# Value sums taken from the attention's own value tiles, in a kernel whose order of work is one written line

## The chip, the cores and the metric

One Trainium2 chip, one core. The metric is device microseconds of one execution. Six things run beside each other on the core: TensorE (PE in the tables, with PEld for its weight loads), VectorE (DVE), ScalarE (ACT), GpSimd (POOL), SyncE (SP, which here only issues DMAs), and the DMA engines themselves. Each of the five engines works through its own instructions strictly in the order in which they were written.

## The reference

Local attention with a coarse summary of the whole sequence, then two dense blocks. Batch 2, 8 heads, 768 positions, head width 64. Each query sees the positions less than 16 away and, besides, 24 summaries of 32 positions each: the maximum of the keys and the mean of the values.

```python
k_sum = k.reshape(B, H, nb, block, D).max(axis=3)      # nb 24, block 32
v_sum = v.reshape(B, H, nb, block, D).mean(axis=3)
scores_l = where(|i - j| < 16, scale * q @ k.T, -1e9)
scores_s = scale * q @ k_sum.T + log(block)
a = softmax(concat([scores_l, scores_s]))
x = a @ concat([v, v_sum])                             # 1536 tokens x 512
h = x @ w_in;  g = max(h, 0) + log1p(exp(-|h|))        # 512 -> 2048
x2 = g @ w_out                                         # 2048 -> 512
out = (((x2 @ w1) * (x2 @ w2)) @ w3) @ w_out2          # 512 -> 1024 -> 512
```

## The kernel before

**Steps and the line.** The work is cut into 2,060 named steps. Every step has an engine, a function that issues its instructions, the steps it needs, and the buffers that it takes and gives back. `LINE` (from line 59) names all steps once, in one order; the last lines of the kernel walk through it and call each function. So the line fixes the order on every engine, SP's queue of DMA issues included. `Order.order` (line 38) only asserts, while the program is built, that needs come first and that no pool of buffers is overdrawn; it issues nothing. The numbers handed to `add` and `padd` (costs, due times, `lead`) were for the search that wrote the line and issue nothing either. The waits on the chip come from the data and the buffers: an instruction waits for what it reads, and the first write to a buffer waits for the last use of the tile that had it.

**Attention.** Twelve tiles of 128 queries, u = 0 to 11, six for each batch element. For tile u: `kw{u}` copies two windows of 96 keys out of the loaded keys `kl`, `ks{u}` adds the 24 block maxima (`km`), `A{u}` makes the scores on TensorE, `max{u}e` (DVE) and `exp{u}e` (ACT) do the softmax in 8 pieces, `inv{u}` (DVE) and `norm{u}h` (POOL) divide, `T{u}h` transposes on TensorE into one of two "a" banks, `at{u}h` copies that out (h = 0 on DVE, h = 1 on ACT), `AV{u}` multiplies with the values, and `xh{u}`, `xl{u}` split the result into two parts for the dense blocks.

**Values.** `vw{u}` loads the two windows of 96 value rows of tile u into rows 0 to 95 of a tile with 120 rows; there are four such tiles. Rows 96 to 119 are the 24 block means. These come from a second load of all the values: `vl{b}{i}`, four transfers of 384 rows each, into a buffer of the "xt" pool (3 buffers). `vs{b}s{i}` multiplies them with a selection matrix (1/32 where a row belongs to a block) on TensorE, 12 products for each half batch. `vsT{b}` copies the sums out on ACT. For batch element 0, `vsu0` turns them back into rows on TensorE and `vs0_h`, `vs1_h` copy them into the tiles of u = 0 and 1; all others go through DRAM (`vss{b}` stores, `vs{u}` loads).

**Dense blocks.** `H` (x @ w_in), `sa` to `lo` (softplus and split), `X` (g @ w_out), products for a Strassen-like scheme (`Ph`, `Pp`), `wm` (w3 @ w_out2), `AB` and `O` (the last product, 24 steps for each column m of four). Every weight passes through a load `l…`, four conversions `ca` to `cd` on ACT and DVE, and `ce`, `c…` on ACT and POOL. At the end `Oo{c}{m}` copies the bank of rows c, m out (odd m on DVE, even m on ACT, into one of 6 "tmp" buffers) and `Os{c}{m}` stores it from SP.

**Order around the change, before.** SP: kl0 ml il q0 kl1 vl00 q1 vw3 sell q2 vw2 kl2 vw0 vl10 vw1 kl3 lw_in0 lw_in2 lw_in1 vl01 q5 q4 q3 vl11. TensorE: A1 A0 vs0s0 A2 T01 T00 T10 T11 T20 T21 vs0s1 vsu0 A3 AV1 AV0 A4 A5 T30. The end of the line: O22_3 Oo10 O23_3 Os10 Oo23 Os23.

Of the kernel before, what the change touches and what calls it, by code (L numbers as in the profile page):

```python
# [59 lines left out]
kl0 sz ml z il busy q0 kl1 vl00 q1 vw3 sell q2 vw2 kl2 vw0 vl10 km0 kw1 vw1 kl3 kw0 lw_in0 lw_in2 lw_in1 km1 kw5 ks0 ks1 ks5 vl01 A1 A0 kw2 max10 q5  # L60
max11 exp10 max12 exp11 vs0s0 max13 kw4 q4 ks2 exp13 max00 exp12 max01 exp00 max02 exp01 max03 max04 exp02 A2 max05 exp03 ks4 max14 exp05 max15 max16
exp15 kw3 q3 max20 exp16 max21 max22 exp14 max23 exp04 max24 max25 exp24 max26 exp25 max27 ks3 exp27 km2 exp23 exp26 exp22 exp20 max17 exp21 max06
max07 exp06 inv2 exp07 norm20 exp17 inv0 vl11 inv1 norm01 norm11 T01 at01 norm21 norm10 km3 norm00 T00 caw_in0 T10 cbw_in0 at10 at00 T11 ccw_in0 T20
cdw_in0 at11 at20 lw_in3 ccw_in1 T21 caw_in1 cbw_in1 at21 caw_in2 cdw_in1 vs0s1 cbw_in2 cew_in1 lw_out0 ccw_in2 vsT0 cw_in1 vss0 vsu0 cdw_in2 vs0_1
vs0_0 lw_out1 A3 vs1_1 vs1_0 cew_in2 AV1 cew_in0 max30 kw6 q6 max31 exp30 max32 max33 exp32 cw_in2 AV0 max34 vw5 exp33 max35 max36 exp34 ks6 exp31 A4
max37 cw_in0 vw4 xh0 exp37 xl0 A5 exp35 q7 kw8 max40 exp36 max41 exp40 vs2 max42 inv3 kw7 q9 exp42 max43 vs3 exp41 max44 max45 exp44 norm31 max46
exp43 max47 max50 exp47 max51 norm30 exp46 max52 max53 exp45 max54 exp53 inv4 T30 exp50 max55 T31 ks8 norm40 exp52 at30 xh1 A6 ks7 at31 vs5 norm41 xl1
# [1127 lines left out]
```

## Time and profile before

| | us |
|---|---|
| median of 3 runs | 576.73 (576.16 to 577.13) |
| the profiled execution's own time | 579.54 |
| its span, first to last instruction | 577.8 |
| TensorE busy in the span | 542.0 (94%) |
| VectorE, ScalarE, GpSimd busy | 440.1, 325.6, 183.1 |

The rows are of that one profiled execution, and their times count from the start of its span. "[8.0 <-POOL s L373]" behind a row says how long the engine had idled before it and what ended the wait. PEclk is the TensorE clock that was granted: 1.00 is 2.4 GHz, 0.50 is 1.2 GHz, and a value between is a mean over a stretch that had both.

### The profile page before, as it was taken

To read this page: it belongs to the slowest core of one execution; us is meant where nothing else is said; L and a number is where in the kernel's file an instruction comes from. 1 tells how busy PE (TensorE), PEld (TensorE's weight loads), DVE (VectorE), ACT (ScalarE), POOL (GpSimd) and SP (SyncE) were. 2 spreads that over 40 slices of the span, in tenths; PEclk is the share of its full clock that TensorE was granted. 3 is DMA by queue.
4 is the path that set the end of the run, shared out by engine and by line. 5 is a ranking of instruction groups with operands and counts; after the bars stand their busy time and mean duration, and the time that the engine had idled before them with its cause. 6 is when DMAs were issued, how large, how long until landed. Compare 5 with 4: busy or idle time off the path is not lost.

```text
span 577.8 us, 8732 instructions
## 1 busy us (share of the span) xinstructions
PE 542.0 (94%) x3118; PEld 441.3 (76%) x3118; DVE 440.1 (76%) x812; ACT 325.6 (56%) x695; POOL 183.1 (32%) x162
## 2 busy tenths in 40 slices
...
GB/s 287 334 272 168 172 111 73 180 169 196 39 145 97 233 163 130 213 243 54 238 223 108 218 250 312 307 206 174 152 127 1 19 73 0 1 1 1 1 1 145
DMA packets 35476, 84.29 MB, mean 146 GB/s; under 512 B 4552, under 2 KB 5000, under 8 KB 35432
## 3 DMA queue, kind: packets, MB, share of 16 engines
...
q8 instruction: 24, 0.39, 0.3%
q14 instruction: 20, 0.16, 0.1%
...
## 4 chain that ended last, share of the span: by engine, by line
PE 45%; DVE 19%; issue 11%; DMA 10%; ACT 9%; POOL 5%; SPq 1%; DVEq 0%; POOLq 0%; ACTq 0%
PE abps L663 19%; PE ops L183 9%; PE xps L183 9%; DVE raw L204 3%; ACT s L361 3%; DVE cv L216 3%; PE hps L183 3%; DMA raw<-in_w_dram 3%; PE wps L183 2%; DMA raw<-in_w_out_dram 2%; POOL w L231 2%; DVE gt L462 2%; DVE tm L449 2%; DMA qt<-in_q_dram 2%; POOL w L534 2%
## 5 line engine op out<-in xcount | busy, mean ns | idle before, releaser
L183 PE MATMUL xps<-gt,w 128*128 128x512 f32 x576 | 137.4, 390 | 1.1 <-DVE gt L462 1.0
L231 POOL TENSOR_TENSOR w<-cv,w 128x512 fp32r<-128x512 f32 x60 | 92.8, 1559 | 139.2 <-ACT w L227 123.9
L183 PEld LDWEIGHTS xps<-gt,w 128*128 128x128 f32 x576 | 107.8, 188 | 24.8 <-DVE gt L462 1.9
L204 DVE SCALAR_TENSOR_TENSOR raw<-raw 128x512 int32<-128x512 int32 x72 | 63.0, 880 | 12.9 <-ACT raw L200 12.6
L183 PE MATMUL hps<-xt,w 128*128 128x512 f32 x288 | 70.2, 394 | 2.0 <-DVE u L675 1.4
L183 PE MATMUL ops<-w,pt 128*128 128x512 f32 x288 | 70.0, 390 | 0.1
L216 DVE SCALAR_TENSOR_TENSOR cv<-cv,raw 128x512 int32<-128x512 int32 x72 | 64.2, 900 | 3.5 <-ACT cv L210 2.0
L183 PEld LDWEIGHTS hps<-xt,w 128*128 128x128 f32 x288 | 53.1, 188 | 14.2 <-DVE u L675 1.8
L183 PEld LDWEIGHTS ops<-w,pt 128*128 128x128 f32 x288 | 54.0, 188 | 12.1 <-DVE pt L561 0.9
L200 ACT ACTIVATE raw<-raw 128x512 int32<-128x512 uint16 x69 | 46.2, 674 | 25.7 <-DMA raw<-in_w_dram 14.7
L484 POOL DMA_DIRECT2D x_d<-xo x36 | 32.9, 1096 | 67.8 <-ACT xo L476 55.4
L675 DVE TENSOR_TENSOR u<-u,abps 128x512 f32<-128x512 f32 x42 | 28.8, 686 | 33.1 <-PE abps L663 19.2
L227 ACT CAST w<-cv 128x512 fp32r<-128x512 f32 x72 | 42.9, 619 | 18.7 <-DVE cv L216 14.8
L669 ACT COPY u<-abps 128x512 f32<-128x512 f32 x42 | 24.6, 587 | 44.7 <-PE abps L663 36.3
L183 PE MATMUL abps<-x2t,w 128*128 128x512 f32 x192 | 44.4, 389 | 0.0
L183 PE MATMUL wps<-w 128*128 128x512 f32 x192 | 44.2, 389 | 0.0
L663 PE MATMUL abps<-t,s 128*128 128x512 f32 x168 | 42.6, 392 | 0.6 <-DVE gt L462 0.6
L361 ACT ACTIVATE s<-s,sm 128x120 f32<-128x120 f32 x96 | 36.8, 386 | 8.9 <-DVE sm L355 8.7
L183 PEld LDWEIGHTS wps<-w 128*128 128x128 f32 x192 | 36.0, 188 | 7.5
L183 PEld LDWEIGHTS abps<-x2t,w 128*128 128x128 f32 x192 | 36.0, 188 | 7.5
L452 ACT ACTIVATE tm<-tm 128x512 f32<-128x512 f32 x48 | 29.4, 628 | 20.3 <-DVE tm L449 20.2
L210 ACT ACTIVATE cv<-raw 128x512 f32<-128x512 f32 x52 | 33.8, 668 | 10.3 <-DMA pk_wo<-cv 3.1
...
## 6 DMA issues: line engine op xcount, KB each, us to landing
raw<-in_w_dram SPq DMA_DIRECT2D x32, 512.0 KB
x_d<-xo POOLq DMA_DIRECT2D x36, 256.0 KB, 5.8
raw<-in_w_in_dram SPq DMA_DIRECT2D x16, 512.0 KB
raw<-in_w_out_dram SPq DMA_DIRECT2D x16, 512.0 KB
vw<-in_v_dram SPq DMA_DIRECT2D x12, 384.0 KB
raw<-in_wo_dram SPq DMA_DIRECT2D x8, 512.0 KB
kt<-in_k_dram SPq DMA_DIRECT2D x4, 768.0 KB
qt<-in_q_dram SPq DMA_DIRECT2D x12, 256.0 KB
```

The lines of the kernel that those rows point to most:

```text
L183: nc.tensor.matmul(ps, lhs(a), rhs(b), start=first and i == 0, stop=last and i == 2)
L200: nc.scalar.activation(r[:, :, 0], r.bitcast(U16)[:, :, 1], AF.Copy, bias=-(0.5 - 2.0 ** -14), scale=2.0 ** -13)
L204: nc.vector.scalar_tensor_tensor(r[:, :, 0], r[:, :, 1], -0x80000000, r[:, :, 0], ALU.bitwise_and, ALU.bitwise_or)
L210: nc.scalar.activation(f(c), h, AF.Copy, scale=2.0 ** -112)
L216: nc.vector.scalar_tensor_tensor(c, c, 3, r[:, :, 0], ALU.logical_shift_left, ALU.bitwise_or)
L227: nc.scalar.copy(w[:, 0], f(cvs[kind, i]))
L231: eng.tensor_tensor(w[:, 1], f(cvs[kind, i]), f(w[:, 0]), ALU.subtract)
L361: nc.scalar.activation(s[:, e], s[:, e], AF.Exp, bias=sm[:, 0, e:e + 1], scale=-1.0, accum_out=sm[:, 1, e:e + 1])
L452: nc.scalar.activation(tm[c, i], tm[c, i], AF.Softplus)
L484: nc.gpsimd.dma_start(x2_d[4 * c + o], xo[c, g, o], accum_op=ALU.add)
L663: nc.tensor.matmul(ps, w[:, a, (o + kk) * P:(o + kk + 1) * P], rhs(b), start=k in (1, 5, 2) and kk == 0 and n == 0, stop=kk == 1 and n == ...
L675: nc.vector.tensor_tensor(tu[z, j, d], tu[z, j, d], bank[z, j, k], ALU.add)
```

## The change

The loads `vl` and their buffers go. The block sums are now made from the window tiles `vw{u}`, which hold the same rows: of each of the two windows of a tile, one selection picks the 64 rows of its own two blocks. `vs{b}s{i}` (4 steps of 12 products) become `vss{u}` (12 steps of 8 products), each needing its `vw{u}`. The selection matrix becomes three small ones, filled by three DMAs of two numbers for each of 64 rows. The tiles of u = 4 to 7 now lie together in one "xt" buffer, held until AV7. The store that was called `vss{b}` is now `vsd{b}`. Users of buffers are told to `Order` more fully, and the whole line is another one.

```diff
-    sel_t = ap_.tile([P, 6, 32], F32, name="sel_t")
+    sel_t = ap_.tile([W, 3, 80], F32, name="sel_t")
...
-        nc.sync.dma_start(vt[b][:, 3 * i:3 * i + 3], v[b, 384 * i:384 * i + 384].rearrange("(a p) c -> p a c", p=P))
...
-                nc.tensor.matmul(vs_t[b][32 * c:32 * c + 32], sel_t[:, a], vt[b][:, a, c * P:(c + 1) * P],
-                                 start=a == 0, stop=a == 5)
+    OFFS = (0, 16, 32)
+    def sel_load(v_):
+        nc.sync.dma_start(sel_t[OFFS[v_]:OFFS[v_] + 64, v_, 46:48], sel[0:64, 0, 0:2])
+    def v_sum(t):
+        b, j = divmod(t, NT)
+        if j == 0:
             vs_t[b] = ph.tile([P, P], F32, tag="h", name="vs_t")
+        for blk, w in enumerate(wins(t)):
+            i = 2 * j + blk
+            s_ = sel_t[:, OFFS.index(64 * i - w), 46 - 2 * i:78 - 2 * i]
             for c in range(4):
+                nc.tensor.matmul(vs_t[b][32 * c:32 * c + 32], s_, vw[t][0:W, blk, c * P:(c + 1) * P],
+                                 start=i == 0, stop=i == 2 * NT - 1)
...
+        if t in (4, 5, 6, 7):
+            if t == 4:
+                four[0] = xt_p.tile([NK, 4, 2, D], F32, tag="xt", name="vw4")
+            vw[t] = four[0][:, t - 4]
+        else:
+            vw[t] = ap_.tile([NK, 2, D], F32, tag="vw", bufs=4, name="vw")
...
-             [(tag, f"h{c}_{i}")], [f"w_in{i}"] + ["xt0"] * (i >= NF - 4))
+             [(tag, f"h{c}_{i}")], [f"w_in{i}", f"xt{c}"])
```

The new line, by engine, where it matters here. SP: ml kl0 kl1 sell0 sell2 q0 q1 vw0 vw4 vw1 il q2 vw3 vw2 sell1 kl2 lw_in0 lw_in1 kl3 lw_in2 q5 q4 vw5 q3 lw_in3 vw6 lw_out0 vsd0 q6 vw7 vw8. TensorE: A0 A1 A2 T00 T01 vss0 vss1 vss2 vss3 vss4 T20 T21 T10 T11 vss5 vsu0 A3 AV0 AV1 A4 vss6 A5 vss7 vss8 T30 AV2 T31 A6 vss9 AV3 T40 T41 A8 A7 T51 vss10 AV4 T50 vss11; later H1_0_3 AV11 H1_2 H1_3 X0_0_0 X0_0_1. DVE around the third tile: max26 inv1 max27 km2 ccw_in0 inv2 caw_in0 caw_in1 cbw_in0 at20 cdw_in0 ccw_in1 km3 at10 cbw_in1 cdw_in1 ccw_in2 caw_in2 cbw_in2 vs0_0 vs1_0 max30. ACT there: exp24 exp27 at21 at01 at11 vsT0. Its end:

```diff
-O22_3 Oo10 O23_3 Os10 Oo23 Os23
+O14_2 Ph23 O15_2 Pl23 O15_0 O23_0 O14_3 O15_3 O14_1 O15_1 O16_1 O18_3 O19_3 O20_3 O21_3 O22_3 O23_2 O23_3 O17_1 O18_1 O19_1 O20_1 O21_1 O22_1 O23_1
+Oo21 Oo22 Oo12 Os22 Os21 Oo20 Os12 Oo10 Oo11 Os20 Os10 Os11 Oo23 Os23 Oo13 Os13
```

## Rows read from the trace of the kernel before

**Rows 1.** Windows by stage: length, busy time (instructions) by engine, PEclk, DMA share, GB/s

```profile
core 0: us, PE busy (x) PEld busy (x) DVE busy (x) ACT busy (x) POOL busy (x), PEclk, DMA share, GB/s
...
51.70:99.20 47.50, 44.62 (x704) 37.22 (x705) 41.53 (x161) 43.35 (x153) 22.93 (x26) 1.00 0.48 123
99.20:573.30 474.10, 468.79 (x2053) 383.81 (x2052) 365.38 (x523) 258.21 (x448) 140.53 (x102) 1.00 0.47 132
```

**Rows 2.** Timeline of TensorE, 12 to 60 us: start, length, what, count, wait

```profile
13.01 0.88 PE L343 MATMUL sc<-kw,qt 64*64 64x120 f32 x12 [3.74 <-DMA qt<-in_q_dram]
...
26.31 1.11 PE L381 MATMUL tr<-id_t,s 128*120 128x128 f32 x4 [7.99 <-POOL s L373]
30.31 1.96 PE L381 MATMUL tr<-id_t,s 128*120 128x128 f32 x8 [2.90 <-POOL s L373]
...
35.89 1.01 PE L293 MATMUL vs_t<-vt,sel_t 128*32 128x128 f32 x24
38.97 1.27 PE L302 MATMUL vs_p<-vsT,id_t 128*24 128x128 f32 x8 [2.07 <-ACT vsT L297]
40.16 1.88 PE L343 MATMUL sc<-kw,qt 64*64 64x120 f32 x32
...
51.67 1.09 PE L381 MATMUL tr<-id_t,s 128*120 128x128 f32 x8 [3.23 <-POOL s L373]
...
59.42 1.52 PE L293 MATMUL vs_t<-vt,sel_t 128*32 128x128 f32 x48
```

**Rows 3.** Timeline of ScalarE and of GpSimd in the same stretch

```profile
15.24 0.39 ACT L361 ACTIVATE s<-s,sm 128x120 f32<-128x120 f32 x1 [8.18 <-DVE sm L355]
24.23 0.18 ACT L361 ACTIVATION_READ_ACCUMULATOR s<-s,sm 128x1 f32 x1
43.34 0.39 ACT L361 ACTIVATE s<-s,sm 128x120 f32<-128x120 f32 x1
...
25.27 4.99 POOL L373 TENSOR_TENSOR s<-s,sm 128x480 f32<-128x480 f32 x5 [0.41 <-DVE sm L367]
```

**Rows 4.** Timeline of VectorE: `km1`, the maxima of the second key load

```profile
9.67 1.75 DVE L257 TENSOR_REDUCE ks<-kt 128x48 f32<-128x1536 f32 x1 [2.61 <-DMA kt<-in_k_dram]
```

**Rows 5.** Windows of the first 30 us, columns as in rows 1

```profile
0.00:10.00 10.00, 7.75 (x26) 2.96 (x26) 2.08 (x2) 3.03 (x5) 1.23 (x7) 1.00 0.81 282
10.00:20.00 10.00, 5.31 (x120) 4.63 (x120) 6.95 (x49) 4.76 (x25) 3.81 (x10) 0.83 1.07 303
20.00:30.00 10.00, 1.11 (x4) 0.70 (x4) 6.64 (x17) 5.00 (x25) 5.72 (x6) 0.63 1.03 355
```

**Rows 6.** DMA issues of the first 100 us: size of one

```profile
vw<-in_v_dram SPq DMA_DIRECT2D x12, 384.0 KB
kt<-in_k_dram SPq DMA_DIRECT2D x4, 768.0 KB
qt<-in_q_dram SPq DMA_DIRECT2D x12, 256.0 KB
vt<-in_v_dram SPq DMA_DIRECT2D x4, 768.0 KB
raw<-in_w_in_dram SPq DMA_DIRECT2D x5, 512.0 KB
...
mask_t<-in_mask_dram SPq DMA_DIRECT2D x1, 180.0 KB
```

**Rows 7.** The end: SP's and VectorE's timelines, and DMA rates from 540 us on

```profile
569.86 4.57 SPq L701 DMA_DIRECT2D out_dram<-osb  x8
...
573.38 0.69 DVE L696 COPY osb<-ops 128x512 f32<-128x512 f32 x1 [4.97 <-PE ops L183]
...
GB/s 0 0 0 0 0 0 9 0 0 0 17 0 0 0 0 0 0 0 0 0 0 0 0 0 0 0 0 0 0 0 0 0 261 375 384 384 386 384 35 0
```

**Rows 8.** Waits of TensorE, 100 to 560 us: first and last of five

```profile
PE abps L663 <- DVE pa L554: 1.5, 1, 1.5
...
PE hps L183 <- DVE gt L462: 0.5, 1, 0.5
```

More of the change, by code (lines that the diff above doesn't have):

```diff
@@ L59 @@
 LINE = """
[L60 to L67, printed above, removed]
@@ L144 @@
-O17_3 O18_1 O19_1 O20_1 O21_1 O22_1 O23_1 O20_2 O21_2 O22_2 O23_2 O18_3 Oo22 O19_3 Oo12 Oo21 Os22 Os12 Oo13 Oo20 O20_3 Os21 Oo11 Os20 O21_3 Os13 Os11
-O22_3 Oo10 O23_3 Os10 Oo23 Os23
+z ml kl0 sz busy kl1 sell0 sell2 q0 q1 vw0 vw4 vw1 il q2 vw3 vw2 sell1 kl2 km0 kw1 lw_in0 lw_in1 kl3 lw_in2 kw0 km1 kw2 ks2 ks0 ks1 A0 A1 max00 kw3 q5
+max01 exp00 max02 exp01 max03 kw5 q4 exp02 max04 exp03 max05 vw5 max10 exp04 ks3 ks5 exp05 max06 max07 exp06 max11 exp07 max12 exp11 inv0 exp10 max13
+norm01 max14 exp13 A2 max15 exp12 max16 exp15 norm00 max17 exp16 max20 q3 exp17 max21 kw4 max22 exp21 T00 max23 exp22 max24 T01 exp23 at00 exp20 vss0
@@ new lines @@
+max25 exp14 ks4 vss1 max26 exp25 inv1 exp26 vss2 max27 norm11 exp24 vss3 exp27 km2 vss4 norm10 ccw_in0 inv2 caw_in0 norm20 caw_in1 cbw_in0 norm21 T20
+at20 cdw_in0 T21 ccw_in1 lw_in3 km3 at21 at01 T10 T11 at10 at11 cbw_in1 cdw_in1 vw6 vss5 ccw_in2 lw_out0 vsT0 caw_in2 cew_in1 vsu0 vsd0 cbw_in2
+cew_in0 cw_in1 A3 vs0_1 vs0_0 caw_in3 vs1_0 AV0 cw_in0 q6 vs1_1 max30 max31 vw7 exp30 max32 AV1 kw6 vw8 exp31 max33 vs3 xh0 max34 vs2 max35 exp32 A4
+xl0 vs5 exp35 vw9 max36 exp33 vs4 max37 vss6 exp36 kw7 max40 q8 exp37 max41 A5 max42 exp34 max43 exp42 ks7 inv3 xh1 vss7 kw8 q7 max50 exp50 xl1 exp40
@@ new lines @@
+norm30 max51 exp43 max44 vss8 max45 exp44 norm31 max46 exp45 T30 max47 exp46 max52 ks6 exp47 AV2 at30 exp52 exp51 ks8 max53 exp41 max54 T31 exp53 vw10
+inv4 xh2 A6 max55 norm41 max56 at31 xl2 exp56 vss9 q11 max57 norm40 exp54 max60 AV3 exp57 max61 max62 exp55 kw10 max63 exp62 inv5 T40 exp63 vw11 max64
+norm50 max65 exp64 T41 max66 exp65 A8 max67 xh3 cdw_in2 norm51 exp66 A7 at41 q10 kw11 exp60 xl3 lw_out3 exp61 T51 at40 q9 exp67 kw9 vss10 cew_in2 inv6
+max70 AV4 caw_out0 norm60 ks9 exp70 max71 max72 exp71 T50 norm61 max73 xh4 max74 vss11 exp73 xl4 cw_in2 exp74 max75 vsT1 exp72 H0_0_0 at50 vsd1 exp75
@@ L321, in wins @@
         return [min(max(64 * i - 16, 0), S - W) for i in (j, j + 1)]
+    four = {}
     def vw_load(t):
@@ L731, in fused_kernel @@
     tile_a(1)
-    pe("vs", "vs0s0")
+    pe("vs", "vss0")
+    pe("vs", "vss1")
     tile_a(2)
-    pe("vs", "vs0s1")
+    for i in range(2, 6):
+        pe("vs", f"vss{i}")
     for u in range(T):
@@ L908, in fused_kernel @@
         add(f"q{u}", "SP", 1.0, -7.5 if u == 0 else None, lambda u=u: q_load(u), (), [("q", f"q{u}")], lead=2)
[L909 removed]
+        add(f"vw{u}", "SP", 1.5, None, lambda u=u: vw_load(u), (u in (5, 6, 7) and f"vw{u-1}",),
+            [("vw", f"vw{u}")] if u // 4 != 1 else [("xt", "vw4")] if u == 4 else (), lead=2)
         add(f"ks{u}", "DVE", .3, None, lambda u=u: kw_sum(u), (f"kw{u}", f"km{2*b+1}"), port=True)
```

191 lines of the change are left out of this document (90 added, 101 removed).

## The prediction

> **What bounds the kernel now.** I read the windows by stage first. From 51.7 us on TensorE is the bound: 44.6 of 47.5 us busy up to 99.2, and 468.8 of 474.1 us from there to its last product at 573.3 [rows 1]. What is gained or lost before 50 us goes straight to the end, unless a later stage gives it back; what is saved on another engine after 52 us is worth nothing. Then the timeline of TensorE over the first 60 us, which shows one hole [rows 2]. The scores of three tiles start at 13.0; the first transposes wait until 26.3 and 30.3 for the divisions on POOL; `A3` starts only at 40.2, behind six transposes, `vs0s1` and `vsu0`. ScalarE says the same: 24 exponentials from 15.2 to 24.4, the next one at 43.3 [rows 3]. Last the first 30 us by windows: the DMA engines never idle there, 282, 303 and 355 GB/s [rows 5], so every early landing is a sum of bytes.
>
> **What goes.** Four loads of 768 KB [rows 6], 3.15 MB, some 10 us of the queue at 303 GB/s [rows 5]. Nothing waits for `vl01` itself: `vs0s1` started at once behind the last transpose, at 35.89 [rows 2]. So the gain isn't the transfer, it is what now stands earlier in the queue, and the order of the first three tiles. I follow the new line to `A3`.
>
> **Start.** `km1` began at 9.67 [rows 4]. Queued up to kl1 were 2.1 MB, and 9.67 us at 282 GB/s [rows 5] moved 2.7: a load lands when some 0.65 MB queued behind it have moved too. (The first product, at 13.01, waited for q1 [rows 2], with 3.1 MB queued and 3.7 moved: the same.) Now ml, kl0 and kl1 come first, 1.76 MB [rows 6]; with 0.65 that is 8.5 us. `km1` 1.75 [rows 4], three `ks` of about 0.2: `A0` at 10.9 instead of 13.0, since q0 and q1 follow kl1 at once. The first exponential came 2.2 after the first product [rows 2, 3], now at 13.1; 24 of them took 9.2 [rows 3], so they end at 22.3.
>
> **Three tiles.** Before, the pieces of all three tiles were mixed, so all six divisions came after the last exponential, 1.0 us each on POOL, until 30.3 [rows 3]; six transposes at about 1.0 followed [rows 2]. Now tile 0 goes first: its `inv`, two divisions and T00, T01 fall inside the exponentials (T00 at about 18.8), as do the divisions of tile 1, and vss0 to vss4 fill TensorE while it waits. What is left after 22.3 is tile 2, and it is not quick: on DVE `km2` (1.75) and a conversion stand ahead of `inv2`, which ends at 24.4. Its divisions end at 25.4 and 26.4. T20 runs at 25.4, `at20` copies it by 27.2. T21 takes the bank that `at20` gave back, then `at21` on ACT, `at01` behind it, T10 and T11 behind those: 1.0 for each transpose [rows 2] and about 0.6 for each copy brings T11 to an end at 30.5. The term for this stage is a chain of four transposes and copies instead of six divisions and six transposes.
>
> **The added wait.** `vss5` needs vw5, the 23rd transfer, 8.6 MB with it [rows 6]; with 0.65 that is 9.3 MB, of which 5.85 have moved at 20 us, and the rest at 355 GB/s takes 9.7 [rows 5]: 29.7. With twice the lag 31.6. It meets T11 at 30.5. Queued behind it on TensorE are `vsu0`, `A3` and everything else. `vss5` about 0.7, `vsT0` 0.3, `vsu0` 1.3 [rows 2]: `A3` at 32.8 instead of 40.2, **7.4 earlier**. Ends: 9 if the transposes take half and vw5 lands early, 5.5 if vw5 lands at 31.6 and a copy queues. Before, `vsT0` also stood behind a conversion on ACT (the 2.07 wait [rows 2]); now it goes ahead of it. On DVE five conversions end at 33.6 ahead of `vs0_0`, so exp30 comes at about 35.8 instead of 43.3 [rows 3], again 7.5.
>
> **From A3 to 99 us.** The sums of batch element 1 were 48 products in 1.52 us [rows 2] and become 96 of the same form: **+1.5** on TensorE (0 to 1.5; vss6 to vss8 stand ahead of T30, where it waited 3.23 [rows 2], so part may be hidden). That wait itself should shrink, since all pieces of tile 3 now run before tile 4: between 0 and 3.2, and I take **-1.0**, near the low end, because ACT is busy 43.4 of 47.5 us there [rows 1] and hands the wait on. The chain of batch element 1 (`vss11`, `vsT1`, four stores `vsd1`, the load `vs6`, `AV6`) has about 6.5 us of TensorE work beside it and needs about as much, so at nothing, with 1 us as its price if ACT lags. H1_2 and H1_3, moved ahead of X0_0, cost nothing in themselves and cover the softplus of the first blocks.
>
> **After 99 us.** The amount of work is the same, only the order differs. TensorE's waits from 100 to 560 us add up to 5.0 in five groups [rows 8]. The same kinds remain (H0_13 still directly behind `C12h5` and `lo0_12`, Pp1 still behind a bank that `Pb7` gives), so I put the change at 0, ends -2.5 and +2.5. That buffers have truer users changes no instruction.
>
> **The end.** Here the new line loses. Before, eight stores issued from 569.86 on, 3.4 us ahead of the last product, and the copy behind that product (573.38) was the only one left on DVE [rows 7]; the transfers ran at 384 GB/s up to 576.3, and the span ended at 577.8. In the new line the last product is O23_1, and `Oo21`, its copy, is the first of DVE's four; `Os21` is second in SP's queue, with Os12, Os20, Os10 behind it, whose data are long ready. So one store goes early and seven start after T, the end of TensorE: `Oo21` 0.7, issue and start 0.7, seven times 262 KB at 384 GB/s 4.8, and 1.4 from the last byte to the end as before: T + 7.6 against T + 4.5, **+3.1** (2.5 to 4; `Oo13` waits for a buffer that `Os21` gives back, but the queue is still full then).
> The Trainium skill (DMA: Bandwidth & Descriptors, Specifications) gives 358 GB/s as the limit of one core at the HBM. The trace disagrees: 384 held over the last 4 us [rows 7]. By the page the seven stores would take 5.1 instead of 4.8, and the term would be 3.4.
>
> **The sum.** -7.4 + 1.5 - 1.0 + 0 + 3.1 = -3.8 us. On the span: 577.8 to 574.0. The profiled execution lay 1.7 outside its span and 2.8 above the median of the runs; I take the difference off the median: 576.7 - 3.8 = 573.0 (rounded).
>
> **Rivals.** *More of the hole is filled (faster).* TensorE ran at half clock through much of the hole, 0.63 in the mean from 20 to 30 us [rows 5]; a pair of transposes took 1.96 there and 1.09 at full clock [rows 2]. Now there are vss0 to vss4 and the earlier tiles in it. If the clock stays at 2.4 GHz, four transposes lose 1.7, vw5's landing becomes the limit at about 30, `A3` begins at 32 and runs in 1.0 instead of 1.9, as do the next two steps: some 3 us more, 570. For it: TensorE is never idle for as long as the 8.0 us that it was [rows 2]. Against it: the transposes of tile 2 leave gaps again.
> The Trainium skill (TensorE: Matmul & The Clock Gate, Part 1) says that activity releases the throttle and idling brings it back, which is this rival's mechanism; the rows agree as to direction only.
> *The tail is not what I read (faster).* If the stores went out early after all, the 3.1 would be missing: 570 as well.
> *VectorE takes the place (slower).* Between max30 and lo0_0, which X0_0 waits for, the new line has 133 DVE steps instead of 127, six more conversions and softplus steps of 0.6 each, about 3.5 us. From 51.7 to 99.2 DVE was busy 41.5 of 47.5 us [rows 1]: 6.0 idle, of which 2.5 would be left. But X0_0 now stands two H further back on TensorE, 24 products of 0.23 [rows 1], 5.4 us, so DVE may idle 7.9, 1.9 more than before. Each microsecond beyond that goes to the end. At 11.7 the gain of 3.8 is gone, and at 14 the time is 579. For it: DVE is the fullest engine beside TensorE there, and its waits are for others. Against it: its spare time grows rather than shrinks.
> *vw5 late (no change).* Each us that it lands after 30.5 moves `A3` one to one; at 34.3 nothing is left. That needs 240 GB/s after 20 us instead of 355 [rows 5].
>
> **How the numbers follow.** Forecast 0.46 (own range 571.2 to 575.2); the faster rivals 0.24 together (about 570); vw5, or lost waits that eat the gain, 0.14 (575.6 to 577.9); VectorE or another new wait after 99 us 0.16 (578 to 581). A measurement of this kernel can tell about 0.2%, 1.15 us, from no change. So faster 0.70, same 0.14, slower 0.16. The range 569.3 to 578.0 leaves out about 0.08 below and 0.11 above.
>
> **What would show it.** A3 at 32 to 34 behind `vss5`, exp30 near 36; the T30 wait under 3; TensorE's last product near 566.5 in the profiled span, with about 7.5 us behind it and seven stores issued after it. Wrong if `A3` is later than 35, if TensorE's waits after 100 us come to more than 8, or if the end is as short as before.

## The result, and the profile of the kernel after

The changed kernel took 584.69 us (582.67 to 586.36, 4 runs) beside 576.44 (576.08 to 577.13, 4 runs) for the kernel before: ratio 1.014, 95% interval 1.0106 to 1.0174. Run again later, beside other kernels, it took 586.03 beside 577.93, ratio 1.0135 (1.0100 to 1.0171). It is slower by some 8 us, where 3.8 less was forecast; the range 569.3 to 578.0 missed it.

The two profiled spans account for 4.9 of it (577.8 and 582.7). "Lead" below means how much earlier TensorE is than in [rows 2] and [rows 1] at the same point of its work. At X0_0_0 the line before has X0_0_1 (1.36) already behind it and H1_2 and H1_3 (2.72 each) still to come, so its 100.6 us corresponds to 104.7 in the new line, which starts X0_0_0 at 99.7: lead 5.0. (Starts of single steps, here and in the table of runs, are counted off in the trace along the line.)

| term of the sum | forecast | in the profiles |
|---|---|---|
| A3 starts | -7.4 (at 32.8) | -4.5 (at 35.64) |
| from A3 to X0_0_0 | +1.5 - 1.0 | -0.5 |
| from there to TensorE's end | 0 (-2.5 to 2.5) | +5.9 (573.3 became 574.2) |
| behind TensorE's end | +3.1 (7.6 for 4.5) | +4.0 (8.5 for 4.5) |
| sum | -3.8 | +4.9 |

The first 50 us on TensorE, for [rows 2]:

```profile
start us, us, engine line op out<-in xcount [idle before <-releaser]
...
17.29 1.99 PE L352 MATMUL sc<-kw,qt 64*64 64x120 f32 x32 [4.79 <-DMA qt<-in_q_dram]
19.21 1.96 PE L390 MATMUL tr<-id_t,s 128*120 128x128 f32 x8
21.10 3.24 PE L295 MATMUL vs_t<-vw,sel_t 96*32 96x128 f32 x80
26.03 0.90 PE L390 MATMUL tr<-id_t,s 128*120 128x128 f32 x4 [1.70 <-POOL s L382]
28.40 1.08 PE L390 MATMUL tr<-id_t,s 128*120 128x128 f32 x4 [1.47 <-DVE at L399]
30.15 1.96 PE L390 MATMUL tr<-id_t,s 128*120 128x128 f32 x8 [0.68 <-ACT at L397]
32.34 1.08 PE L295 MATMUL vs_t<-vw,sel_t 96*32 96x128 f32 x16 [0.22 <-DMA vw<-in_v_dram]
33.81 1.90 PE L304 MATMUL vs_p<-vsT,id_t 128*24 128x128 f32 x8 [0.38 <-ACT vsT L299]
35.64 1.46 PE L352 MATMUL sc<-kw,qt 64*64 64x120 f32 x32
...
45.36 0.65 PE L295 MATMUL vs_t<-vw,sel_t 96*32 96x128 f32 x16 [2.60 <-DMA vw<-in_v_dram]
```

The order of events is the forecast one, most of them later. A2's wait of 4.79 us for q2 wasn't in the forecast; T21 waits for `at20`, and `vss5` still 0.22 for vw5, which landed at 32.3. The wait of T30 (3.23 before) has become one of 2.60 of `vss8` for vw8. VectorE in the same stretch shows why `at20` (27.57) is late:

```profile
22.24 1.75 DVE L257 TENSOR_REDUCE ks<-kt 128x48 f32<-128x1536 f32 x1
23.90 0.62 DVE L212 TENSOR_SCALAR cv<-raw 128x512 f32<-128x512 f32 x1
24.45 0.16 DVE L376 TENSOR_SCALAR sm<-sm 128x8 f32<-128x8 f32 x1
...
24.76 1.51 DVE L198 TENSOR_SCALAR raw<-raw 128x512 int32<-128x512 int32 x2
26.18 1.47 DVE L204 SCALAR_TENSOR_TENSOR raw<-raw 128x512 int32<-128x512 int32 x1
27.57 0.68 DVE L399 COPY at<-tr 120x512 f32<-120x512 f32 x1
```

`km2` and a conversion stand ahead of `inv2` (24.45 to 24.84), and three more conversions, 2.7 us, ahead of `at20`.

Waits of TensorE from 100 to 560 us, for [rows 8]: nine groups with 9.0 us in place of five with 5.0. The stage itself, for [rows 1]: 465.9 us busy in 475.0.

```profile
PE hps L183 <- DVE gt L471: 3.1, 5, 1.5
PE abps L183 <- DVE pa L563: 1.5, 2, 1.2
PE abps L672 <- ACT u L678: 1.1, 1, 1.1
PE abps L183 <- ACT w34o L528: 0.7, 1, 0.7
PE wps L183 <- POOL w L231: 0.7, 1, 0.7
PE abps L183 <- POOL w L231: 0.7, 1, 0.7
PE ops L183 <- DVE pt L570: 0.5, 1, 0.5
PE xps L183 <- DVE gt L471: 0.4, 1, 0.4
PE abps L672 <- DVE t L624: 0.3, 1, 0.3
```

The end, for [rows 7]: SP's stores, VectorE's copies, and GB/s from 545 to 583 us in 40 parts.

```profile
569.37 9.77 SPq L710 DMA_DIRECT2D out_dram<-osb  x8
...
574.20 1.89 DVE L705 COPY osb<-ops 128x512 f32<-128x512 f32 x3 [14.34 <-PE ops L183]
577.34 0.69 DVE L705 COPY osb<-ops 128x512 f32<-128x512 f32 x1 [1.25 <-DMA out_dram<-osb]
...
GB/s 0 0 0 0 9 0 0 0 0 0 9 0 0 17 0 0 0 0 0 0 0 0 0 0 0 0 181 95 0 0 0 0 235 371 395 380 380 179 2 0
```

One store goes early, the queue then stands idle until the copy behind the last product, and seven stores follow. The last copy, `Oo13`, waits 1.25 us for the buffer that `Os21` gives back.

### The profile page after: what moved, and what is told of

Its sections match the earlier page's. It is cut to its first block, busy times and chain, and to the rows that moved or that the text cites. A ratio compares the mean times of both kernels' runs of the same rounds, so it can differ in the third digit from the quotient of the medians.

```text
span 582.7 us, 8911 instructions
## 1 busy us (share of the span) xinstructions
PE 549.5 (94%) x3214; PEld 442.4 (76%) x3214; DVE 434.8 (75%) x812; ACT 324.6 (56%) x695; POOL 182.8 (31%) x162
## 3 DMA queue, kind: packets, MB, share of 16 engines
q1 hardware_dynamic: 28104, 71.08, 38.3%
## 4 chain that ended last, share of the span: by engine, by line
PE 38%; DMA 26%; DVE 21%; ACT 9%; issue 4%; SPq 1%; POOL 1%; DVEq 0%; ACTq 0%; POOLq 0%
PE abps L672 15%; PE ops L183 9%; DMA raw<-in_w_dram 6%; PE hps L183 5%; DVE cv L216 4%; PE xps L183 4%; DMA vw<-in_v_dram 4%; DMA cv<-pk_w 4%; DMA raw<-in_w_in_dram 3%; DVE raw L204 3%; DMA raw<-in_w_out_dram 2%; ACT raw L200 2%; PE av L411 2%; DMA pk_wo<-cv 2%; DVE gt L471 1%
## 5 line engine op out<-in xcount | busy, mean ns | idle before, releaser
L204 DVE SCALAR_TENSOR_TENSOR raw<-raw 128x512 int32<-128x512 int32 x72 | 59.2, 829 | 22.9 <-ACT raw L200 22.7
L183 PE MATMUL hps<-xt,w 128*128 128x512 f32 x288 | 71.9, 397 | 3.5 <-DVE gt L471 3.1
L216 DVE SCALAR_TENSOR_TENSOR cv<-cv,raw 128x512 int32<-128x512 int32 x72 | 57.7, 816 | 6.7 <-ACT cv L210 5.0
L183 PE MATMUL abps<-x2t,w 128*128 128x512 f32 x192 | 45.8, 392 | 2.9 <-DVE pa L563 1.5
L183 PEld LDWEIGHTS abps<-x2t,w 128*128 128x128 f32 x192 | 35.6, 188 | 12.2 <-DVE pa L563 2.4
```

The costliest lines, as they stand in the source:

```text
L183: nc.tensor.matmul(ps, lhs(a), rhs(b), start=first and i == 0, stop=last and i == 2)
L204: nc.vector.scalar_tensor_tensor(r[:, :, 0], r[:, :, 1], -0x80000000, r[:, :, 0], ALU.bitwise_and, ALU.bitwise_or)
L216: nc.vector.scalar_tensor_tensor(c, c, 3, r[:, :, 0], ALU.logical_shift_left, ALU.bitwise_or)
```

## The experiments

Two theories at the start. **Order**: the values' change does little; the new line wins at the front and loses in the dense blocks and at the end, each by its own order. **Values**: the changed loads and buffers shift the traffic, and later stages pay whatever their order. "Before" is the median of the kernel before, run beside it on the same chip; starts and ends are those of the profiled execution. X0_0_0 doesn't stand at the same place in all lines: e_swap_dense has it behind H1_2, H1_3 and X0_0_1.

| kernel | us | before | ratio (95%) | A3 | X0_0_0 | TensorE's end | behind it |
|---|---|---|---|---|---|---|---|
| before (profile) | | | | 40.2 | 100.6 | 573.3 | 4.5 |
| after | 584.69 | 576.44 | 1.014 (1.011 to 1.017) | 35.6 | 99.7 | 574.2 | 8.5 |
| before_again | 579.70 | 577.50 | 1.004 (0.998 to 1.009) | 41.5 | 103.7 | 577.2 | 4.5 |
| e_tail | 579.16 | 577.50 | 1.004 (1.000 to 1.008) | 35.4 | 100.4 | 574.0 | 4.0 |
| e_swap_dense | 592.41 | 577.50 | 1.028 (1.023 to 1.033) | 40.6 | 116.0 | 588.9 | 8.0 |
| e_dense_old | 585.09 | 577.50 | 1.012 (1.009 to 1.015) | 35.5 | 99.1 | 578.8 | 5.1 |
| e_values_only | 583.15 | 578.31 | 1.009 (1.006 to 1.012) | 41.6 | 102.1 | 574.3 | 5.1 |
| e_front_after | 575.93 | 578.31 | 0.996 (0.994 to 0.998) | 35.4 | 97.3 | 570.1 | 5.1 |
| e_fix_front | 580.91 | 578.31 | 1.005 (1.002 to 1.008) | 29.7 | 95.0 | 573.4 | 8.6 |
| e_front2 | 574.10 | 578.31 | 0.993 (0.990 to 0.996) | 26.9 | 96.4 | 572.2 | 4.1 |
| e_mid_old | 592.21 | 576.71 | 1.026 (1.020 to 1.033) | 33.3 | 96.7 | 584.1 | 4.1 |
| e_mid_new | 584.75 | 576.71 | 1.013 (1.008 to 1.019) | 34.9 | 98.3 | 574.8 | 8.7 |
| e_blend | 583.92 | 576.71 | 1.012 (1.006 to 1.018) | 33.5 | 106.0 | 579.7 | 4.0 |
| e_blend_late | 580.82 | 576.71 | 1.007 (1.004 to 1.010) | 32.2 | 101.2 | 572.8 | 4.1 |
| e_fix_sp | 586.17 | 577.93 | 1.014 (1.010 to 1.018) | 36.3 | 99.5 | 575.1 | 8.6 |
| e_less_dve | 572.11 | 577.93 | 0.991 (0.986 to 0.995) | 31.4 | 97.0 | 561.5 | 8.6 |
| e_best | 572.27 | 577.93 | 0.991 (0.988 to 0.994) | 29.6 | 94.7 | 565.9 | 4.0 |
| e_best_vl | 575.21 | 577.93 | 0.996 (0.994 to 0.998) | 34.3 | 102.5 | 569.8 | 3.9 |
| e_best_rep | 571.42 | 577.93 | 0.989 (0.986 to 0.992) | 32.8 | 99.0 | 569.0 | 4.1 |
| after_rep | 586.03 | 577.93 | 1.014 (1.010 to 1.017) | 36.2 | 100.7 | 574.7 | 8.6 |

**before_again.** The kernel before, unchanged.

> The kernel before, once more, for a second profile of it. Its profiled execution took 579.54 us while the median of its timed runs was 576.4. If that profile was an unlucky one, the new one has a span of about 574.7 and somewhere in it some 3 us less of waits; then the kernel after the change lost about 8 us against it and not the 5 that the two first profiles show. If profiling itself costs 3 us, the span is 577 to 578 again. Ratio 1.000 within 0.002.

The second profile was worse than the first: span 581.7, A3 at 41.5 and the granted clock at 0.54 from 20 to 40 us, where the first had 0.65. So 577.8 was not an unlucky one. The median of the timed runs lies lower than both, and which waits those runs lack isn't shown; 3 of the 8 us stay without a row.

**e_tail.**

```diff
-O14_2 Ph23 O15_2 Pl23 O15_0 O23_0 O14_3 O15_3 O14_1 O15_1 O16_1 O18_3 O19_3 O20_3 O21_3 O22_3 O23_2 O23_3
+O14_2 Ph23 O15_2 Oo12 Os12 Pl23 O15_0 Oo10 Os10 O23_0 Oo20 Os20 O14_3 O15_3 Oo13 Os13 O14_1 O15_1 Oo11 Os11 O16_1
+O18_3 O19_3 O20_3 O21_3 O22_3 O23_2 Oo22 Os22 O23_3 Oo23 Os23
...
-O23_1 Oo21 Oo22 Oo12 Os22 Os21 Oo20 Os12 Oo10 Oo11 Os20 Os10 Os11 Oo23 Os23 Oo13 Os13
+O23_1 Oo21 Os21
```

> The kernel after the change with its last sixteen steps moved: each copy and store of a result follows the product that completes it, so that only Oo21 and Os21 stand behind the last product. Nothing else differs. Theory (seven stores behind the last product cost what they cost in the trace, 8.5 us from TensorE's end to the end of the span): one store remains, 0.7 for the copy, 0.7 to issue it, 0.7 of transfer, 1.4 to the end, 3.5 to 4.5 together, so 4 to 5 us less than the kernel after the change: 580 to 581. Rival (the end hangs on something else, such as the last stores' own latency): less than 2 us gained, 583 to 585.

579.16 us, and 4.0 us behind TensorE's end. SP's stores and VectorE's last copies:

```profile
560.37 14.77 SPq L710 DMA_DIRECT2D out_dram<-osb  x8
...
569.33 0.69 DVE L705 COPY osb<-ops 128x512 f32<-128x512 f32 x1 [4.80 <-PE ops L183]
574.09 0.69 DVE L705 COPY osb<-ops 128x512 f32<-128x512 f32 x1 [4.07 <-PE ops L183]
```

The stores now begin 14 us ahead of the end, and one is left behind it. The end of the new line cost 4.5 us more than it needed to, as read.

**e_swap_dense and e_dense_old.** The attention of the one line, the dense blocks of the other.

```diff
 lo0_1 X0_0_1
-cdw_out2 lo0_2 cew_out2 lw_in4 ccw_out3 ccw_in5 X0_0_0
+cdw_out2 cbw_in5 ccw_in5 ccw_out3 cdw_out3 lw_in7 cdw_in5 lw_out4
...
```

> The kernel before (values loaded twice, its own order) through X0_0_1, at about 108 us, and from there the new line's order and its end. Theory (the new order of the dense blocks loses 6 us and its end 4, whatever the values do): slower than the kernel before by 9 to 13 us, 585 to 589, and the waits of TensorE from 110 us on come to 9 instead of 5. Rival (what was lost comes from the values' change, for instance from DMA traffic or buffers that it shifts): as fast as the kernel before but for the end, 576 to 581.

```diff
 sa1_3 Xo00_2 H2_0
-sa1_1 sb1_3 cbw_in4 Xs00_2 sb1_1 sc1_3 caw_out5 sc1_1
+cbw_in4 ccw_in4 cdw_in4 cew_in4 cw_in4 sa1_1 Ss1h2 Ss3h2
...
```

> The kernel after the change, with the new line only through H2_0 (about 112 us); from there the order and the end of the kernel before, twelve steps postponed until their buffers are free. Theory (the attention with its values loaded once wins 5 us at 100 us, and the order behind it loses it): 5 us faster than the kernel before, 571 to 572.5. Rival (the attention's gain is given back later in any order, because the later stage waits for loads that an earlier start doesn't bring forward): 575 to 577.

592.41 and 585.09: the first slower than forecast (and its profiled execution, 598.69, slower still), the second not faster at all. Neither decides, because at the seam conversions pile up that the other line had done earlier: TensorE waits 4.1 us there in the one, 3.0 and 1.4 in the other. Its products slow down behind these waits too: in e_dense_old the granted clock is 0.78 from 110 to 125 us and 0.90 from 125 to 144, and the twelve of the step at 123.52 took 5.42 us, where 2.88 is usual. Its lead of 5.6 at X0_0_0 has become a lag of 2.7 at H0_4 and of 5.5 at TensorE's end; what it lost behind the seam, in the old order, isn't explained. From 131 us to TensorE's end the first loses another 6.7.

**e_front_after and e_mid_new** have no such seam. The first is the new line through A3 and then the old order; the second is the first through X1_14_1 (324 us) and then the new order.

```diff
 cew_in0 cw_in1 A3
-vs0_1 vs0_0 caw_in3 vs1_0 AV0 cw_in0 q6 vs1_1
+cdw_in2 vs0_1 vs0_0 lw_out1 vs1_1 vs1_0 cew_in2 AV1
...
```

> The new line through A3 and from there the order of the kernel before (with vss6 to vss11 where vs1s0 and vs1s1 were), to its end. Here no step has to be postponed, unlike in the earlier splice at H2_0, where TensorE lost 4.4 us in two waits at the seam. Theory (the front wins 4.5 us at A3, the new dense order loses 6 and the new end 4): A3 at 35.6, and 572 to 574, some 3 to 4 us less than the kernel before and 11 less than the kernel after the change. Rival (the gain of the front is given back in any order): 576 or more.

```diff
 cw30 sb2_13 X1_14_1
-upw32 lo1_15 cewo23 sc2_13 Xl0_2 cwo20 X1_15_0 upwo24
+upw31 sa2_15 cew31 cewo23 Xl0_2 lo1_15 cwo20 cwo23
...
```

> The reverse: e_front_after's line (new front, dense blocks in the order of the kernel before) through X1_14_1 (324 us), from there the new order and the new end. Theory (the new order of the products w3 @ w_out2 and AB loses 3 to 4 us by waits for weights and its end 4): TensorE ends near 573 instead of 570.1, 8 to 9 us behind it, 582 to 584. Rival (the new order's second part is harmless where the first is the old one): TensorE ends at 570, 578 to 579.

e_front_after ended TensorE at 570.1 and took 2.4 us less than the kernel before. Its lead at X0_0_0, 3.3, is still 3.2 at TensorE's end. e_mid_new took 584.75. Waits of TensorE from 320 to 575 us, first e_front_after, then e_mid_new:

```profile
PE xps L183 <- DVE gt L471: 0.5, 1, 0.5
```

```profile
PE ops L183 <- DVE pt L570: 1.9, 2, 1.3
PE wps L183 <- POOL w L231: 1.8, 2, 1.4
PE abps L183 <- ACT w34o L528: 0.9, 1, 0.9
PE abps L183 <- POOL w L231: 0.4, 1, 0.4
```

The same kernel up to 324 us, 0.5 us of waits in the old order behind it and 5.0 in the new one. From X1_14_1 to TensorE's end it is 245.6 against 251.2. This is the cleanest of the runs on the dense blocks: the order alone costs 5.6 us there. Half of it lies in the products AB. Counting each of TensorE's instructions at 0.227 us, their usual distance, e_mid_new needs 3.4 us more than that from AB00 to AB70, e_front_after 0.6; the kernel after needs 3.6 and the kernel before 0.7.

**e_mid_old**, the reverse: e_fix_front's line through X0_12_0, then the old order.

```diff
 Xs22_0 lo1_12 X0_12_0
-Xs22_1 U2h7 upw34 Ph7_7 X0_13_0 X0_14_1 caw33 cbw33
+Ph2_7 ccw32 cdw32 pkw32 C11h7 caw33 cbw33 upw34
...
```

> e_fix_front's line through X0_12_0 (304 us), from there the order of the kernel before (no step postponed), with the end of e_tail. In e_fix_front A3 was 6 us earlier than after the change and X0_0_0 4.7 earlier, but X0_12_0 started at 303.7 in both: between 115 and 285 us the loads of the weights were issued first 4.6 us earlier and in the end not at all. Theory (the new order has two places that lose: that stage, and the products AB from 350 to 430 us; the second is now taken out): X0_12_0 at 303 to 304 again, no TensorE waits of more than 0.5 us from 320 us on, TensorE ends near 570, 574 to 576.5 in all. Rival (the second loss is no matter of the order but follows from the first): AB waits as in e_fix_front, 577 to 579.

592.21: a miss, by its seam again. `U2h7`, one copy on ScalarE, came to stand behind two conversions whose loads were late, and the product behind it waited 12 us:

```profile
317.74 2.50 PE L672 MATMUL abps<-xt,s 128*128 128x512 f32 x5 [11.99 <-ACT u L678]
```

Behind that, from X1_14_1 on, it took 248.1 us, close to the 247.3 of the kernel before, without the waits of e_mid_new. That part fits the order theory; the total says nothing.

**e_values_only.** The values' change in the old order.

```diff
-T01 at01 norm21 norm10 km3 norm00 T00
+T01 at01 norm21 norm10 km3 norm00 vss0 vss1 vss2 vss3 vss4 T00
...
```

> The values' change alone, in the order of the kernel before: the vl loads give their places in SP's queue to vw4, vw5 and vw6, the sums are made by vss0 to vss4 ahead of T00 and vss5 where vs0s1 was, vss6 to vss11 where vs1s0 and vs1s1 were; nothing else moves. Theory (the values' change itself is worth little, since A3 hangs on the order of the first three tiles and TensorE has 3 us more of sums): A3 at 38 to 41, and the whole within 2 us of the kernel before, 575 to 579. Rival (the shorter queue of loads is what brings A3 forward): A3 at 34 to 36 and 571 to 573.

583.15, 0.9% slower than the kernel before and slower than either theory said. Its profiled execution (span 579.4) has A3 at 41.6 and TensorE's end at 574.3, about as the kernel before, so the values' change in the old order brings A3 no earlier; `vsu0` waits 2.86 us there for `vsT0`. The other 2 to 4 us of the timed runs aren't in that profile, and why this kernel is slower isn't shown; e_front_after, with the same change of the values, is not.

**e_fix_front and e_fix_sp.** What made A3 later than 32.8?

```diff
-q0 q1 vw0 vw4 vw1 il q2 vw3 vw2 sell1 kl2
+q0 q1 q2 vw0 vw4 vw1 il vw3 vw2 sell1 vw5 kl2
...
-km2 vss4 norm10 ccw_in0 inv2 caw_in0 norm20 caw_in1 cbw_in0 norm21 T20 at20
+inv2 norm20 norm21 km2 T20 at20 vss4 norm10 ccw_in0 caw_in0 caw_in1 cbw_in0
...
```

> The kernel after the change with eight steps moved ahead of A3 and nothing behind it: q2 directly behind q1 and vw5 ahead of kl2 in SP's queue; inv2, the divisions of tile 2, T20 and at20 ahead of the conversions on DVE. Theory (A3 was 2.8 us later than predicted because q2 and vw5 were issued late, each SP load waiting for the eighth load before it, and because at20 stood behind a conversion of 1.5 us): q2 is no longer waited for 4.8 us by A2, vss5 doesn't wait, and A3 starts at 31 to 33 instead of 35.6, the whole 2.5 to 4 us below the kernel after the change, 580 to 582. Rival (the landings are set by the bytes ahead alone, whatever the order of issue): A3 at 34.5 to 36 and no measurable gain.

e_fix_sp is the first hunk alone.

```diff
-q0 q1 vw0 vw4 vw1 il q2 vw3 vw2 sell1 kl2
+q0 q1 q2 vw0 vw4 vw1 il vw3 vw2 sell1 vw5 kl2
...
```

> The kernel after the change with two loads moved in SP's queue and nothing else: q2 directly behind q1, vw5 ahead of kl2. It splits e_fix_front, which also moved inv2, the divisions of tile 2, T20 and at20 ahead of conversions on DVE. Theory (the two late landings and the conversion ahead of at20 each hold A3 up): A2 at 12 to 13, vss5 without a wait for vw5, at20 at 26.5 to 27.5 still behind a conversion, A3 at 32.5 to 34, between 35.6 and the 29.7 to 33.5 of e_fix_front's front. Rival (landings alone): A3 at 30 to 32. Rival (the conversion alone): A3 at 35 or later.

With both hunks A3 starts at 29.65 (29.6 to 33.5 in the seven runs that have this front), with the loads alone at 36.3. In e_fix_sp A2 no longer waits for q2 and `vss5` not for vw5, but VectorE does:

```profile
23.39 1.75 DVE L257 TENSOR_REDUCE ks<-kt 128x48 f32<-128x1536 f32 x1 [3.66 <-DMA kt<-in_k_dram]
...
25.39 0.17 DVE L376 TENSOR_SCALAR sm<-sm 128x8 f32<-128x8 f32 x1
...
28.53 0.68 DVE L399 COPY at<-tr 120x512 f32<-120x512 f32 x1
```

kl2 lands later since vw5 went ahead of it, `km2` waits 3.66 us, and `inv2` and `at20` stand behind `km2`. Earlier landings of q2 and vw5 are worth nothing while VectorE's order is as it is. What the second hunk gives alone wasn't run.

The whole: 580.91, within the expectation and by the ratios some 5 us better than the kernel after. The profiled execution (583.75, above its median) shows a place where such a lead is lost: 4.7 us at X0_0_0, nothing at X0_12_0, which starts at 303.7 as in the kernel after, and 0.8 at TensorE's end. Part of that may be chance: behind a wait of 2.02 us 12 products of H0_15 took 4.61 us at a lower clock, 3.02 in the kernel after.

**e_less_dve.** What takes it back? This kernel, in e_fix_front's line, leaves out the second conversion step of each weight, on VectorE, 72 steps in all (the expectation says 64); the weights lose their signs.

```diff
-        nc.vector.scalar_tensor_tensor(r[:, :, 0], r[:, :, 1], -0x80000000, r[:, :, 0], ALU.bitwise_and, ALU.bitwise_or)
```

> e_fix_front without the second of the four conversion steps of every weight, the one on DVE that merges the sign (0.69 us each, 64 of them); the signs of the weights are left out of the sums. Everything else and the order are as in e_fix_front. There X0_0_0 started 4.7 us earlier than after the change and X0_12_0 at the same time. Theory (from 115 to 285 us the loads of weights wait on SP for conversions on DVE, 118 of 180 us in the trace of after, so that this chain and not TensorE sets the pace): with 0.69 less on DVE for each weight X0_12_0 starts at 298 to 301.5 instead of 303.7 and TensorE's waits from 200 to 285 us fall from 4.5 to under 2. Rival (the chain is the landing time of the loads, 4 to 7 us each): X0_12_0 at 303 or later.

X0_12_0 at 295.9 in place of 303.7, AB10 at 384.5 in place of 393.3, TensorE's end at 561.5 in place of 573.4; by the ratios the whole takes 1.4% less than e_fix_front. Waits of TensorE from 100 to 560 us, all of them, and the window 200 to 285 us:

```profile
PE wps L183 <- POOL w L230: 1.2, 1, 1.2
PE hps L183 <- DVE gt L470: 0.9, 2, 0.7
PE abps L671 <- DVE t L623: 0.2, 1, 0.2
```

```profile
200.00:285.00 85.00, 85.00 (x375) 70.11 (x374) 60.87 (x101) 57.97 (x105) 28.52 (x27) 1.00 0.74 183
```

In the kernel after, the same window reads

```profile
200.00:285.00 85.00, 82.07 (x358) 66.51 (x358) 68.73 (x116) 55.78 (x101) 25.06 (x24) 1.00 0.70 175
```

and in e_fix_front, with which e_less_dve shares its line,

```profile
200.00:285.00 85.00, 80.27 (x341) 64.21 (x340) 66.22 (x112) 53.61 (x97) 25.19 (x24) 0.98 0.66 165
```

With 0.69 us less on VectorE for each weight TensorE never idles there. So in the new order VectorE's load is what holds TensorE up behind 100 us, and the landing times are not. The conversions are the part of it that was taken off; other work of VectorE wasn't tried. The gain is larger than expected, since the waits of the AB stage go too. That the same cut would gain less in the old order wasn't tried. SP's waits for these conversions don't tell the two orders apart: from 110 to 290 us they are 117.6 us in both kernels. Which exchanges in the new order do the harm is open.

**e_front2.** A front by hand, the old order behind it. Shown are SP's and TensorE's own steps, picked out of the lines of the kernel after (-) and of this one (+).

```diff
-q0 q1 vw0 vw4 vw1 il q2 vw3 vw2 sell1 kl2
+q0 q1 q2 il vw0 vw1 vw2 sell0 sell2 sell1 vw3 vw4 vw5 kl2 q3
...
-T00 T01 vss0 vss1 vss2 vss3 vss4 T20 T21 T10 T11 vss5 vsu0 A3
+T00 T01 vss0 vss1 vss2 T10 T11 vss3 vss4 T20 T21 vss5 vsu0 A3
...
```

> A front written anew by hand on the same reasons, then the order of the kernel before with the conversions of the first three weights spread over tiles 3 to 5, and the end of e_tail. SP: kl0 kl1 ml q0 q1 q2 il vw0 to vw5 with the sel loads between, then kl2 and q3; at01 directly behind T01 so that both transpose banks come back at once; T00 T01 T10 T11 T20 T21 in this order, vss between. Theory: exponentials of three tiles without a gap to 21.8, A3 at 27 to 29, and 565 to 570 in all. Rival (VectorE and ScalarE, which have only 6 and 4 us of 47 to spare from 52 to 99 us, take the place, since the conversions no longer fit into a hole): A3 at 27 to 29, but X0_0_0 at 97 or later instead of 92 to 94, and 572 to 576.

574.10; A3 at 26.9, a little earlier than expected, but X0_0_0 at 96.4, near the rival's 97: from A3 to there it took 69.5 us, the kernel before 60.5. The longest wait on the way, on TensorE, then GpSimd:

```profile
43.12 1.96 PE L390 MATMUL tr<-id_t,s 128*120 128x128 f32 x8 [9.99 <-POOL s L382]
```

```profile
40.40 1.27 POOL L231 TENSOR_TENSOR w<-cv,w 128x512 fp32r<-128x512 f32 x1 [1.28 <-ACT w L227]
41.63 1.43 POOL L382 TENSOR_TENSOR s<-s,sm 128x480 f32<-128x480 f32 x1
```

A weight's last conversion on GpSimd, waiting for its two forerunners on ScalarE and VectorE, stood ahead of the division that T30 needs. That is 2.5 us of the wait: the division before it ended at 39.13, and this one began at 41.63. What held the rest isn't resolved, so the rival stands.

**e_blend and e_blend_late.** The attention of e_fix_front, the dense steps where the old line has them, from T40 and from T90 on.

```diff
 exp62 inv5 T40
-exp63 vw11 max64 norm50 max65 exp64 T41 max66
+cdw_in2 lw_out1 cew_in2 cw_in2 exp63 vw11 max64 norm50
...
```

> e_fix_front's line through T40; from there its order of the attention's steps, but every step of the dense blocks (loads and conversions of weights included) where the order of the kernel before has it, counted in steps of TensorE's attention; the end of e_tail. Theory (the attention in the new order with q2 and vw5 early is worth 8 to 10 us, and only the new dense order gives them away): A3 at 29.7, TensorE ends at 563 to 567, 567 to 572 in all, less than every kernel so far. Rival (a start that early is given back in the old dense order too, since the loads and conversions of the weights bound that stage): waits at H0_13 of 3 us and more, TensorE ends at 569 or later, 573 to 576.

```diff
 cdw_out2 exp107 T90
-inv11 T91 lw_out1 inv10 norm111 caw_in5 H1_1_0 at90
+lw_out1 ccw_out1 sa0_1 caw_out1 cbw_out1 inv11 T91 cdw_out1
...
```

> As e_blend, but the new line's own order, with its loads and conversions, through T90 (about 80 us), so that VectorE and ScalarE have the new line's load during the attention. Theory: 567 to 573 as e_blend. Rival (the new line's early loads of weights from 50 to 100 us are themselves what makes the dense stage late): 3 us and more above e_blend.

583.92 and 580.82, both misses: conversions, some of them late for their loads, came to stand inside the attention, TensorE waited 5.3 us for divisions in the one and 6.2 for one copy in the other, and the lead was gone before the dense blocks began. From X0_0_0 to TensorE's end they took 473.7 and 471.7, the kernel before 472.7.

**e_best.** The attention untouched; the loads and conversions of weights in the old order only from its end on.

```diff
 AV10 cdw_out3 cew_out1
-lw_in7 cdw_in5 H1_0_1 lw_out4 cw_out1 xh10 cew_out2 T110 xl10 cew_out0 lw_in6 T111
+cdw_in5 H1_0_1 cw_out1 xh10 cew_out2 T110 xl10 cew_out0 T111
...
 hi0_1 X0_0_1 hi0_2 lo0_1
-ccw_in6 lo0_2 cew_out3 X0_1_1 lo1_0 caw_in7 cw_out3 caw_in6 cbw_in7 X0_1_0
+lo0_2 cew_out3 X0_1_1 lo1_0 cw_out3 X0_1_0 lw_in4 lw_in7 caw_in4 lw_out6 cbw_in4
...
```

> e_fix_front's line through AV11 and the first products X0_0 (the attention, H0 to H1 with H1_2 and H1_3 ahead of X0_0), without the loads and conversions of weights that the kernel before has later; from there the order of the kernel before, and the end of e_tail. In the two earlier blends the conversions of the dense blocks stood in a heap inside the attention (T90 and AV9 waited 3 and 6 us); here the attention keeps its own. Theory (the new attention is some 8 us ahead at X0_0 and only the new dense order gives that away): X0_0_0 at 93 to 98, TensorE ends at 562 to 568, 3.5 to 4.5 us behind it, 567 to 573 in all. Rival (the old dense order can't use an early start either, because loads and conversions of weights are a second bound of that stage): H0_13 waits 4 us or more, TensorE ends at 569 or later, 574 to 577.

> e_best once more, on the chip of e_best_vl and of the kernel after the change: 571 to 574, 0.7 to 1.2% below the kernel before; A3 at 29.6 to 33.5, with the granted clock from 20 to 40 us high where it is early.

572.27 and 571.42, 0.9 and 1.1% less than the kernel before and 2.5% less than the kernel after (586.03, run beside e_best_rep): it beats both. Leads at X0_0_0 and at TensorE's end, against the first profile of before:

| dense order | kernel | at X0_0_0 | at TensorE's end |
|---|---|---|---|
| new | after, after_rep, e_fix_sp | 5.0, 4.0, 5.2 | -0.9, -1.5, -1.8 |
| new | e_tail, e_fix_front | 4.3, 9.7 | -0.7, -0.1 |
| new, less on VectorE | e_less_dve | 7.7 | 11.8 |
| old | e_front_after, e_front2 | 3.3, 4.2 | 3.2, 1.1 |
| old | e_best, e_best_rep, e_best_vl | 10.0, 5.7, 2.2 | 7.4, 4.2, 3.5 |

In these single profiles the new order gave back 5 to 7 us, and 9.8 in e_fix_front, whose timed runs kept more than that; the old one gave back 3.1 at most (e_best_vl gained 1.3), and of e_best's 10 us it kept three quarters. Kernels in which TensorE waited at a seam are left out.

**e_best_vl.** e_best with the values loaded twice. The second piece shows TensorE's steps alone.

```diff
-q2 vw0 vw4 vw1 il vw3 vw2 sell1 vw5 kl2
+q2 vw0 vl00 vw1 il vw3 vw2 vl01 kl2
...
-T10 T11 vss5 vsu0
+T10 T11 vs0s1 vsu0
...
```

> e_best's order with the values loaded twice as before the change: vl00, vl01, vl10, vl11 where vw4 to vw7 were, the sums by vs0s0 and vs0s1 (24 products each) where vss2 and vss5 were, by vs1s0 and vs1s1 where vss10 and vss11 were, vw4 to vw11 behind the AV that frees their buffer. It tells what the values' change is worth in a good order. Theory (the order is what counts): within 2 us of e_best, 570.5 to 574.5; A3 0 to 2 us later, since 0.8 MB more stands ahead of the sums, and 3 us less of sums on TensorE. Rival (the saved transfer is what lets the front start early): A3 at 34 or later and 577 or more.

> The kernel after the change once more, beside e_best: 582 to 586, 10 to 13 us above e_best; A3 at 35 to 36, TensorE's end at 573 to 576 and 8 to 9 us behind it.

575.21 beside 571.42: in a good order the values' change is worth 3.8 us by the medians, more than the theory's 2 and less than the rival's 5 and more. T21 waits 3.82 us there and 1.54 in e_best_rep, A3 starts 1.5 us later and X0_0_0 3.5. (The spans differ by 0.6 only; e_best_rep's profiled execution took 574.88, 3.5 more than its median.) The order alone, with the values as before, is worth 2.7. after_rep is as expected.

## Why the prediction was wrong

**The start and the three tiles: right in kind, too small by 2.9.** T00 first, the divisions of the first tiles hidden, a chain of transposes and copies behind tile 2: as described. I had `inv2` behind `km2`, and it ended at 24.84, close to the 24.4 worked out. But I let `at20` follow T20 at once; the line that I had copied out has three conversions between `inv2` and `at20`, and they took 2.7 us. T21, T10 and T11 moved with it (T11 ended at 32.1, not 30.5). vw5 landed at 32.3, not 29.7 (254 GB/s moved from 10 to 20 us, where 303 had been taken), and it hardly mattered, since T11 ended at the same time. So of the 2.8 us by which A3 was late, 1.6 were there at T11's end and 0.2 are the wait for vw5. The last 1.0 came behind it: at a granted clock of 0.50 (30 to 36 us) `vss5` took 1.08 and `vsu0` 1.90, where I had put 0.7 and 1.3. With e_fix_front's front A3 started at 29.6 to 32.2 in four runs, better than I claimed, and at 32.8 to 33.5 in three; e_fix_sp shows that earlier landings of q2 and vw5 alone don't bring it. The stated bound, A3 later than 35, was crossed, and exp30 came at 38.3, not 35.8.

**From A3 to 99 us: right** (+0.5 forecast, -0.5 found); the wait that I took to shrink from 3.23 became one of 2.60 for vw8.

**After 99 us: the step that failed.** "The amount of work is the same, only the order differs ... so I put the change at 0." The only evidence was the small waits of the old order [rows 8]. Those waits were small because that order fitted, not because the stage was loose: VectorE was busy 365.4 of 474.1 us [rows 1]. A line written anew had everything there to lose. I set the ends at 2.5, half of the waits that were there; the price was 5.9, and 5.6 from 324 us alone in e_mid_new. The stated bound, waits of more than 8, was crossed (9.0). The waits make 4.0 of the 5.9; the rest is in products that follow one another more slowly than at the usual 0.227 us. By place, as time over 0.227 us an instruction: from AB00 to AB70 it is 3.6 where the kernel before has 0.7; from H0_12 to X0_12_0 it is 4.1 where that has 1.7, but before_again has 3.7 and e_front_after 3.6, so this part can't be put down to the order. A premise fell with the step, "what is saved on another engine after 52 us is worth nothing": in e_less_dve, time saved on VectorE alone brought TensorE's end from 573.4 to 561.5 (in the new order; the old one wasn't tried).

**The rival that came true, in another place.** "VectorE or another new wait after 99 us" had 0.16 and 578 to 581. I had worked it out for VectorE between max30 and lo0_0, where it left TensorE its lead. It took the place behind 100 us, where time taken off VectorE's conversions comes back (e_less_dve). The time lies above its 578 to 581: the start and the end were dearer than that price had them, and 3 us stay without a row.

**The end: right in kind, 0.9 too small.** Seven stores behind the last product, as read, and `Oo13`'s wait for `Os21`'s buffer was hidden, as I had it: 379 GB/s moved from 575.75 to 580.5 us. What the sum lacked is a tail: from 580.75 to 581.25 the last bytes came at 20 GB/s, some 0.5 us of the 0.9. Why isn't shown; the rest is in small differences of start and end.

**Clock stays full (rival): the clock fell here as before**, 0.67 from 20 to 30 us for 0.63 [rows 5].

**The values.** I took the 3.15 MB for room in the queue and didn't ask what the order alone would give. In the old order the values' change brought A3 no earlier and made the kernel 0.9% slower; in e_best's it is worth 3.8 us, and the order 2.7.
